# Routed attention and a two-layer network on one Trainium2 core: the up-projection by Strassen's seven products, its left factors streamed from memory

## The chip, the core and the metric

The kernel runs on one NeuronCore of a Trainium2 chip. The core has five engines that run their own instruction streams: TensorE (PE in the profile; its weight loads are listed apart as PEld), VectorE (DVE), ScalarE (ACT), GpSimd (POOL) and SyncE (SP), which here only starts DMA transfers. They meet through semaphores. The metric is the device time of one execution in microseconds. The kernel before took 1125.86 us (median of three runs, 1125.33 to 1126.34).

## What is computed

Inputs are q, k, v of shape (4 batches, 8 heads, 768 rows, 64), 16 centroids for each head, and two weight matrices, w_in (512 x 2048) and w_out (2048 x 512), which arrive as 64-bit floats.

```python
q_assign = argmax(q_n @ c_n.T); k_assign = argmax(k_n @ c_n.T)      # q, k, centroids normalized
scores   = where(q_assign == k_assign, q @ k.T / sqrt(64), -1e9)
attn     = softmax(scores) @ v                                       # per batch and head
x        = attn.transpose(0, 2, 1, 3).reshape(3072, 512)
h        = x @ w_in
g        = h - tanh(h)
out      = g @ w_out                                                 # (3072, 512)
```

## The kernel before, in words

All work is in 32-bit floats. The 3072 tokens are eight **blocks** of 384 (a batch, `b`, and a half of its rows, `half`). Heads go in pairs `p` (4 pairs of 2 heads, one above the other in the 128 partitions). For a block the attention is 12 **steps**: 4 pairs by 3 thirds `s` of the keys; 96 steps in all, in the order of `steps` (line 445). The program is written in its final order by hand: what stands first in the code stands first in each engine's queue.

A step k emits the following (loop from line 524):

- `begin` (line 489): the scores of step k+1, two tiles j0 and j1 (128 keys each, both heads), each followed by an exponential on ACT that overwrites the tile in PSUM (`score`, line 317). The two tiles take both buffers of the pool `ps_s`.
- `value` (line 350): the products of step k's weights with v; in a pair's last third `total` (line 377) multiplies the weights' sum with ones on PE (the tile `den`), which needs the sums that POOL keeps (`sum`, lines 344 and 348).
- items of the **fill**: the network of the block before. `ffn_items` (line 406) gives 16 items `up` (four matmuls over the 512 inputs, 128 x 384 each, then tanh on ACT and `h - tanh` on DVE, line 422) and 12 items `project` (four matmuls of 128 x 512, line 428). The last block's network has no attention beside it and runs alone at the end (lines 568 to 572).
- the list `todo` of the step, cut in equal parts over the slots `between` that each item offers: the two `select` of step k+1 (DVE compares codes and multiplies, line 335; two instructions a tile; the second one also emits POOL's sums), then now and then the transposes of a coming pair (`turn`, line 238, which uses the same two `ps_s` buffers), `divide` (the reciprocal of the sums, line 399), `weights_on`, `route` and `publish` (the arg-max codes).

`weights_on` first turns the 64-bit weights to 32 bits (32 pieces, lines 117 to 125; one piece a step in block 0, three a step in block 1), and then loads each piece again to test its smallest value (line 165). The weights stay in SBUF. Loads of q, k and v go through SP, 8 transfers outstanding at most; the weights' loads go through POOL.

The 16 `up` of a block come in its first six steps (3, 3, 3, 3, 2, 2 to a step), the 12 `project` in the last six, two to a step. Blocks are numbered from 0; in the profile block 2 runs from 265.7 to 391.9 us, and in it the network of block 1.

Of the kernel before, what the change touches and what calls it, by code (L numbers as in the profile page):

```python
# [28 lines left out]
F32 = mybir.dt.float32  # L29
BF16 = mybir.dt.bfloat16  # L30
I32 = mybir.dt.int32
U32 = mybir.dt.uint32
ALU = mybir.AluOpType
# [3 lines left out]
P = 128  # L37
# [14 lines left out]
def kernel(  # L52
# [10 lines left out]
    nc = tc.nc  # L63
# [30 lines left out]
    wholes = const.tile([P, TB], F32, name="wholes")  # L94
    smallest = const.tile([P, len_pieces], F32, name="smallest")
    flag = const.tile([1, 1], I32, name="flag")
    w_in = [const.tile([P, CD, FQ * P], F32, name=f"w_in{i}") for i in range(NQ4)]
    w_out = [const.tile([P, FQ, DM], F32, name=f"w_out{i}") for i in range(NQ4)]

    out_r = out.rearrange("(b p j) m -> b j p m", p=P, j=NCH)  # L100
# [1 line left out]

    w_in_r = moe_w_in.rearrange("(c p) f -> p c f", p=P)
    w_out_r = moe_w_out.rearrange("(c p) m -> p c m", p=P)
    PIECES = [
        (w_in[i][:, c], w_in_r[:, c, i * FQ * P * words : (i + 1) * FQ * P * words])
        for i in range(NQ4) for c in range(CD)
    ] + [(w_out[c // FQ][:, c % FQ], w_out_r[:, c]) for c in range(CF)]

    def assemble(dst, raw, rest):  # L110

# [13 lines left out]
        nc.vector.tensor_tensor(out=bits, in0=bits, in1=rest, op=ALU.add)  # L125

    def fast():
        loads = cx.enter_context(tc.tile_pool(name="loads", bufs=2))
        vp = cx.enter_context(tc.tile_pool(name="vp", bufs=4))
        turnp = cx.enter_context(tc.tile_pool(name="turnp", bufs=4))  # L130
        rtp = cx.enter_context(tc.tile_pool(name="rtp", bufs=1))
        codep = cx.enter_context(tc.tile_pool(name="codep", bufs=6))
        qbp = cx.enter_context(tc.tile_pool(name="qbp", bufs=4))
        ep = cx.enter_context(tc.tile_pool(name="ep", bufs=2))
        sump = cx.enter_context(tc.tile_pool(name="sump", bufs=2))
        xp = cx.enter_context(tc.tile_pool(name="xp", bufs=2))
        rawp = cx.enter_context(tc.tile_pool(name="rawp", bufs=3))
        thp = cx.enter_context(tc.tile_pool(name="thp", bufs=2))
        gp = cx.enter_context(tc.tile_pool(name="gp", bufs=4))
        outp = cx.enter_context(tc.tile_pool(name="outp", bufs=2))  # L140
        ps_s = cx.enter_context(tc.tile_pool(name="ps_s", bufs=2, space=PSUM))
        ps_a = cx.enter_context(tc.tile_pool(name="ps_a", bufs=1, space=PSUM))
        ps_f = cx.enter_context(tc.tile_pool(name="ps_f", bufs=3, space=PSUM))

        raws = {}

        def fetch_weights(n: int):
# [7 lines left out]
        def round_weights(n: int):  # L155
            if words == 1:
                return
            rest = outp.tile([P, FQ * P], U32, name="rest", tag="osb")
            assemble(PIECES[n][0], raws.pop(n), rest)

        def check_weights(n: int):
# [61 lines left out]
        def load(n: int, what=(0, 1)):  # L223
            if n >= len(pairs):
                return
            b, p = pairs[n]
            for i in what:
                if i < 2:
                    t = raw_qk[n, i] = loads.tile([P, NCH, 2, D], F32, name=f"x{i}")
                else:  # L230
                    t = vals[n] = vp.tile([P, 2, NCH, D], F32, name="vals")
                for h in range(2):
                    nc.sync.dma_start(
                        t[:, :, h] if i < 2 else t[:, h],
                        (q, k, v)[i][b, 2 * p + h].rearrange("(p j) d -> p j d", p=P),
                    )
# [166 lines left out]
                nc.gpsimd.tensor_tensor(out=inverses, in0=inverses, in1=dens.pop((n, half)), op=ALU.add)  # L403


        def ffn_items(b: int, half: int):
            gs, acc = [], {}

            def up(f: int, between):
                i, o = f // FQ, f % FQ  # L410
                if o == 0:
                    gs.append(gp.tile([P, FQ, TB], F32, name="g"))
                h = ps_f.tile([P, TB], F32, name="h", tag="f")
                for c in range(CD):
                    nc.tensor.matmul(  # L415
                        h, lhsT=w_in[i][:, c, o * P : (o + 1) * P], rhs=xT[b, half][:, c],
                        start=(c == 0), stop=(c == CD - 1),
                    )
                th = thp.tile([P, TB], F32, name="th")
                nc.scalar.activation(out=th, in_=h, func=ACT.Tanh)  # L420
                between()
                nc.vector.tensor_tensor(out=gs[i][:, o], in0=h, in1=th, op=ALU.subtract)  # L422

            def project(sub: int, i: int, between):
                if i == 0:
                    acc[sub] = ps_f.tile([P, DM], F32, name="o", tag="f")
                for o in range(FQ):
                    nc.tensor.matmul(  # L428
                        acc[sub], lhsT=gs[i][:, o, sub * P : (sub + 1) * P], rhs=w_out[i][:, o],
                        start=(i == 0 and o == 0), stop=(i == NQ4 - 1 and o == FQ - 1),  # L430
                    )
                between()
                if i == NQ4 - 1:
                    osb = outp.tile([P, DM], F32, name="osb")
                    nc.scalar.copy(out=osb, in_=acc.pop(sub))  # L435
                    nc.gpsimd.dma_start(out_r[b, half * HCH + sub], osb)  # L436

            return [lambda between, f=f: up(f, between) for f in range(CF)] + [
                lambda between, s=s, i=i: project(s, i, between)
                for s in range(HCH) for i in range(NQ4)  # L440
            ]

# [6 lines left out]

        def before(n: int):  # L450

            yield lambda: (turn(n, 0, nc.scalar), turn(n, 1, nc.scalar), load(n + 2))
            yield lambda: similar(n)
            yield lambda: route(n)
            yield lambda: publish(n)
# [17 lines left out]
        def fetch():  # L473
            nonlocal fetched
            if fetched < (1 if words == 1 else 2) * len(PIECES):
                fetch_weights(fetched % len(PIECES))
                fetched += 1

        def weights_on():

            nonlocal done
            if done < len(PIECES):
                round_weights(done)
            elif done < 2 * len(PIECES) and words == 2:
                check_weights(done - len(PIECES))
            done += 1
            fetch()

        def begin(step):
            n, half, s = step  # L490
            for i in range(2):
                score(n, half, 2 * s + i)

        centroid_load()
        load(0)
        for i in range(3):
            fetch()
        constants()
        load(1)
        load(0, (2,))  # L500
        for n in range(1, HP):
            load(n, (2,))
        turn(0, 0, nc.scalar)
        turn(0, 1, nc.vector)
        centroid_norms()
        similar(0)
        turn(1, 0, nc.scalar)
        load(2)
        route(0)
        publish(0)  # L510
        spread(0, 0)
# [3 lines left out]
        for i in range(2):  # L515
            select(*steps[0][:2], i)
        turn(1, 1, nc.scalar)
        load(3)
        similar(1)
        route(1)  # L520
        publish(1)

        late = []
        for at, (n, half, s) in enumerate(steps):
            b, p = pairs[n]
            following = steps[at + 1] if at + 1 < len(steps) else None
            after = steps[at + 2] if at + 2 < len(steps) else None
            block = 2 * b + half
            if p == 0 and s == 0:
                fill = ffn_items((block - 1) // 2, (block - 1) % 2) if block else []  # L530
            left = HP * NS - (p * NS + s)
            now = [fill.pop(0) for _ in range(-(-len(fill) // left))]
            stages = dict(ready.get(at, []))
            if 1 in stages:
                stages[1]()
            if after and after[2] == 0:
                spread(*after[:2])
            if following:
                begin(following)
            value(n, half, s)  # L540
            if s == NS - 1:
                total(n, half)
                late += [lambda n=n, half=half, i=i: divide(n, half, i) for i in range(HCH)]
                if half == 1:
                    load(n + HP, (2,))

            todo = []
            if following:
                todo += [lambda i=i: select(*following[:2], 2 * following[2] + i) for i in range(2)]
            if 0 in stages:  # L550
                todo.append(stages[0])
            todo += late
            late = []
            todo += [weights_on] * (3 if block == 1 and done < len(PIECES) else 1)
            todo += [stages[i] for i in (2, 3) if i in stages]
            slots = max(len(now), 1)
            for i in range(slots):
                mine = todo[i * len(todo) // slots : (i + 1) * len(todo) // slots]

                def between(mine=mine):  # L560
                    for it in mine:
                        it()

                if i < len(now):
                    now[i](between)
                else:
                    between()
        fill = ffn_items(B - 1, 1)
        for it in late:
            it()  # L570
        for it in fill:
            it(lambda: None)


        for t, bound in ((inverses, MOST_INVERSE), (wholes, SUM_MOST)):
# [16 lines left out]
    def general():  # L592
# [3 lines left out]
        identb = gs.tile([P, P], BF16, name="identb")  # L596
        nc.vector.tensor_copy(out=identb, in_=ident)

        for dst, src in PIECES if words == 2 else ():
            raw = gs.tile([P, 2 * FQ * P], U32, name="graw")  # L600
            nc.sync.dma_start(raw, src)
            rest = gs.tile([P, FQ * P], U32, name="grest")
# [165 lines left out]
```

## Time and profile before

| | |
|---|---|
| median of three runs | 1125.86 us |
| the profiled execution, its own time | 1126.44 us |
| its span (first to last instruction) | 1124.5 us |
| PE busy | 1063.1 us, 95% |
| DVE, ACT, POOL busy | 509.9, 304.7, 377.9 us |
| matmuls of `up` (line 415) | 344.0 us |
| matmuls of `project` (line 428) | 341.0 us |
| DMA, mean | 59 GB/s |

How to read it: the page cuts the span into 40 slices and gives each engine's busy share of a slice in tenths. A float matmul goes through PE in two passes and is listed as two instructions, each with a weight load of its own. `x24` after an operation is a count of such instructions that were merged in one row. In a row of the timeline the first number is the start, the second the length in us; in square brackets stands the engine's idle time ahead of it and what ended it. The view by windows gives busy us and instruction counts of each engine in a stretch, then the clock that PE was granted (1.00 is full), and the share of the DMA engines.

### The profile page before, as it was taken

The numbers are of one execution on the slowest core, as the hardware profiler recorded it, in microseconds if no ns is written. First come the engines' busy times: TensorE is split into PE (matmuls) and PEld (weight loads), VectorE is DVE, ScalarE is ACT, GpSimd is POOL, SyncE is SP. The second block draws the span as 40 slices with busy tenths as digits, with TensorE's granted clock in tenths as the row PEclk, the third lists the DMA queues.
The fourth block names the chain that finished last, engine by engine and source line by source line (L and its number), as shares of the span: only waits on it lengthen the run. The fifth ranks groups of instructions, "written<-read, shape, count | busy, mean of one in ns | idle before, by whom it ended". The sixth has DMA issues, their size and how long they took to land.

```text
span 1124.5 us, 10709 instructions
## 1 busy us (share of the span) xinstructions
PE 1063.1 (95%) x3922; PEld 500.6 (45%) x3922; DVE 509.9 (45%) x893; ACT 304.7 (27%) x491; POOL 377.9 (34%) x298
## 2 busy tenths in 40 slices
PE   3776998999999999999999999999999999999996
PEld 2332444444544455444554445444554445444542
DVE  3578899534553344444543234443343334432210
ACT  2333334322322223222332223313332122211100
POOL 1012344443353433434234333343334433442000
PEclk9988999999999999999999999999999999999999
DMA  7442256433222123331100002110000000000000
GB/s 197 122 115 77 78 158 183 139 98 92 79 64 66 63 64 88 91 104 62 36 29 10 10 9 50 38 43 30 12 28 10 24 10 1 1 10 19 1 9 22
DMA packets 71115, 65.86 MB, mean 59 GB/s; under 512 B 53136, under 2 KB 61328, under 8 KB 71056
## 3 DMA queue, kind: packets, MB, share of 16 engines
q0 software_dynamic: 11136, 39.85, 11.1%
q1 hardware_dynamic: 59776, 25.22, 9.1%
q8 instruction: 33, 0.54, 0.2%
q14 instruction: 26, 0.21, 0.1%
q10 hardware_dynamic: 144, 0.03, 0.0%
HBM read 58.75 MB, written 6.34 MB: 58 GB/s over the span
## 4 chain that ended last, share of the span: by engine, by line
PE 78%; issue 9%; DVE 9%; DMA 1%; ACT 1%; POOL 1%; SPq 0%; POOLq 0%; DVEq 0%; ACTq 0%
PE o L428 26%; PE h L415 23%; PE sc L321 12%; PE av L357 11%; PE sim L261 2%; DVE e L335 2%; PE den L385 1%; DVE w_out L122 1%; PE pt L243 1%; DVE den L399 1%; ACT t L249 1%; PE den L366 1%; DMA x<-in_k_dram 1%; DVE w_out L125 1%; DVE w_out L118 1%
## 5 line engine op out<-in xcount | busy, mean ns | idle before, releaser
L415 PE MATMUL h<-xT,w_in 128*128 128x384 f32 x1024 | 344.0, 492 | 5.8 <-DVE top L282 4.0
L428 PE MATMUL o<-w_out,g 128*128 128x512 f32 x768 | 341.0, 598 | 0.0
L335 DVE SCALAR_TENSOR_TENSOR e<-row,code,sc 128x384 f32<-128x384 bf16 x384 | 211.7, 607 | 254.4 <-ACT sc L326 195.7
L348 POOL TENSOR_TENSOR sum<-sum,e 128x768 f32<-128x768 f32 x112 | 202.5, 1808 | 260.1 <-DVE e L335 257.4
L415 PEld LDWEIGHTS h<-xT,w_in 128*128 128x128 f32 x1024 | 191.6, 191 | 157.1 <-issue 19.2
L428 PEld LDWEIGHTS o<-w_out,g 128*128 128x128 f32 x768 | 142.4, 190 | 188.5 <-issue 183.4
L326 ACT ACTIVATE sc<-sc 128x768 f32<-128x768 f32 x192 | 144.4, 793 | 208.4 <-PE sc L321 194.2
L321 PE MATMUL sc<-t,t 64*128 64x384 f32 x768 | 155.8, 524 | 5.8 <-DVE e L335 5.5
L422 DVE TENSOR_TENSOR g<-h,th 128x384 f32<-128x384 f32 x128 | 71.0, 554 | 184.3 <-ACT th L420 184.0
L357 PE MATMUL av<-e,vals 128*64 128x384 f32 x768 | 148.5, 508 | 0.0
L420 ACT ACTIVATE th<-h 128x384 f32<-128x384 f32 x128 | 62.7, 490 | 300.6 <-PE h L415 298.5
L321 PEld LDWEIGHTS sc<-t,t 64*128 64x128 f32 x768 | 68.1, 191 | 83.8 <-issue 56.6
L399 DVE RECIPROCAL den<-den 128x128 f32<-128x128 f32 x96 | 84.0, 919 | 35.6 <-POOL wholes L393 35.6
L357 PEld LDWEIGHTS av<-e,vals 128*64 128x64 f32 x768 | 47.4, 138 | 89.9 <-issue 87.2
L393 POOL TENSOR_TENSOR wholes<-wholes,den 128x384 f32<-128x384 f32 x32 | 31.8, 993 | 139.3 <-ACT den L392 139.3
L436 POOL DMA_DIRECT2D out_dram<-osb x24 | 13.3, 553 | 156.5 <-ACT osb L435 156.5
L403 POOL TENSOR_TENSOR inverses<-inverses,den 128x384 f32<-128x384 f32 x32 | 43.7, 1364 | 63.4 <-DVE den L399 63.4
L435 ACT COPY osb<-o 128x512 f32<-128x512 f32 x24 | 14.1, 588 | 168.6 <-PE o L428 168.6
L344 POOL TENSOR_TENSOR sum<-e 128x768 f32<-128x768 f32 x28 | 50.4, 1802 | 5.1 <-DVE e L335 5.1
L153 POOL DMA_DIRECT2D raw<-in_moe_w_in_dram x32 | 18.3, 571 | 88.7 <-DVE w_in L122 60.1
L249 ACT COPY t<-pt 128x768 f32<-128x768 f32 x31 | 23.5, 801 | 69.9 <-PE pt L243 69.9
L243 PE MATMUL pt<-ident,x 128*128 128x128 f32 x192 | 27.0, 293 | 15.4 <-DMA x<-in_q_dram 9.6
(67 smaller groups left out, 372.2 us busy)
## 6 DMA issues: line engine op xcount, KB each, us to landing
raw<-in_moe_w_in_dram POOLq DMA_DIRECT2D x32, 512.0 KB, 4.3
raw<-in_moe_w_out_dram POOLq DMA_DIRECT2D x32, 512.0 KB, 4.0
x<-in_q_dram SPq DMA_DIRECT2D x32, 192.0 KB
x<-in_k_dram SPq DMA_DIRECT2D x32, 192.0 KB
vals<-in_v_dram SPq DMA_DIRECT2D x32, 192.0 KB
row<-q_codes SPq DMA_DIRECT2D x32, 192.0 KB
out_dram<-osb POOLq DMA_DIRECT2D x24, 256.0 KB, 2.3
q_codes<-qc SPq DMA_DIRECT2D x16, 3.0 KB
```

The costliest lines, as they stand in the source:

```text
L321: nc.tensor.matmul(sc[:, h, 0:TB], lhsT=turned[n, 1][r].rearrange("p a n -> p (a n)")[:, j * P : (j + 1) * P], rhs=turned[n, 0][r, half], ...
L326: nc.scalar.activation(out=sc[:, :, 0:TB], in_=sc[:, :, 0:TB], func=ACT.Exp, scale=SCALE)
L335: nc.vector.scalar_tensor_tensor(out=e[:, h], in0=rows[n, half][:, h], scalar=codes[n][:, 1, j // HCH, h, j % HCH : j % HCH + 1], in1=sc[: ...
L344: nc.gpsimd.tensor_tensor(out=s, in0=pair[:, 0], in1=pair[:, 1], op=ALU.add)
L348: nc.gpsimd.tensor_tensor(out=s, in0=s, in1=pair[:, i], op=ALU.add)
L357: nc.tensor.matmul(avs[n, half][h * D : h * D + D], lhsT=vals[n][:, h, j], rhs=e[:, i, h], start=(j == 0), stop=(j == NCH - 1),)
L399: nc.vector.reciprocal(out=t[:, c], in_=t[:, c])
L403: nc.gpsimd.tensor_tensor(out=inverses, in0=inverses, in1=dens.pop((n, half)), op=ALU.add)
L415: nc.tensor.matmul(h, lhsT=w_in[i][:, c, o * P : (o + 1) * P], rhs=xT[b, half][:, c], start=(c == 0), stop=(c == CD - 1),)
L420: nc.scalar.activation(out=th, in_=h, func=ACT.Tanh)
L422: nc.vector.tensor_tensor(out=gs[i][:, o], in0=h, in1=th, op=ALU.subtract)
L428: nc.tensor.matmul(acc[sub], lhsT=gs[i][:, o, sub * P : (sub + 1) * P], rhs=w_out[i][:, o], start=(i == 0 and o == 0), stop=(i == NQ4 - 1 ...
```

## The change

For the blocks 1 to 7 the up-projection is done on quarters. Two outputs f and f+8 of 128 features each and the two halves of the block's 384 tokens (192 each) make a 2 x 2 product, and the 512 inputs are halved. Seven products of (128 outputs) x (256 inputs) x (192 tokens) replace eight. The seven left factors (four of them sums of quarters of w_in) are made once, in block 1 after the weights are done, by DVE; they are written to DRAM and read back by SP, one tile `stream` of 7 KB a partition for each pair of outputs, three pairs ahead. Four differences of the quarters of x are made by DVE at each block's end. So an item `up_pair` holds 14 matmuls of 128 x 192 in place of 8 of 128 x 384; the products are put together by one copy on ACT and four additions on DVE, with tanh on ACT and the subtraction now on POOL. Block 0's network still uses `up`, with one buffer for tanh's result where there were two.

The fill is dealt out by estimated cost (2.6 for `up`, 4.6 for `up_pair`, 3.4 for `project`) in place of item counts. An `up_pair` offers two slots to `todo`, one ahead of its last two products' addition and one at its end. Buffers are rearranged: q and k of batch 0 sit in the buffers of g and are all loaded at the start; later ones have one buffer in place of two and are loaded one pair ahead; `row` has three buffers in place of four. At the start the identity is made ahead of the first weight loads on POOL. The second reading of the weights starts at block 2 (before: in block 1).

```diff
+        def keep_factor(q: int, which: int, t):
+            for c in range(CH):
+                nc.sync.dma_start(
+                    factors[q * FQ : (q + 1) * FQ, :, which, c].rearrange("i p f -> p i f"),
+                    t[:, c].rearrange("p (i f) -> p i f", f=P),
+                )
+        def factor_items(q: int):
...
+            return [
+                lambda: (make(S1, a21, a22, ALU.add), keep_factor(q, A11, a11)),
+                lambda: (make(S3, a11, a21, ALU.subtract), keep_factor(q, A12, a12)),
+                lambda: (make(S2, S1, a11, ALU.subtract), keep_factor(q, S1, made[S1])),
+                lambda: (keep_factor(q, S3, made[S3]), make(S4, a12, S2, ALU.subtract)),
+                lambda: (keep_factor(q, S2, made[S2]), keep_factor(q, A22, a22)),
+                lambda: keep_factor(q, S4, made[S4]),
+            ]
+        def fetch_factors(k: int):
+            if k < (2 * B - 1) * HF:
+                t = streams[k] = wp.tile([P, 7, CH, P], F32, name="stream", tag="w")
+                nc.sync.dma_start(t, factors[k % HF])
+        def differences(b: int, half: int):
...
+            for i, (u, w) in enumerate(((b12, b11), (b22, d[:, 0]), (b22, b12), (b21, d[:, 1]))):
+                nc.vector.tensor_tensor(out=d[:, i], in0=u, in1=w, op=ALU.subtract)
...
+            def up_pair(i: int, between):
...
+                m = mixp.tile([P, 8, N], F32, name="mix", tag="mix")
+                ps = ps_f.tile([P, N], F32, name="p1", tag="f")
+                product(ps, A11, x[:, 0:CH, 0:N])
+                nc.scalar.copy(out=m[:, 7], in_=ps)
+                ps = ps_f.tile([P, 2, N], F32, name="p26", tag="f")
+                product(ps[:, 0], A12, x[:, CH:CD, 0:N])
+                product(ps[:, 1], S2, d[:, 1])
+                nc.vector.tensor_tensor(
+                    out=m[:, 0:7:6], in0=ps, in1=m[:, 7:8].to_broadcast([P, 2, N]), op=ALU.add
+                )
+                ps = ps_f.tile([P, 2, N], F32, name="p75", tag="f")
+                product(ps[:, 0], S3, d[:, 2])
+                product(ps[:, 1], S1, d[:, 0])
+                nc.vector.tensor_tensor(out=m[:, 5], in0=ps[:, 0], in1=m[:, 6], op=ALU.add)
+                nc.vector.tensor_tensor(
+                    out=m[:, 3:5], in0=ps[:, 1:2].to_broadcast([P, 2, N]), in1=m[:, 5:7], op=ALU.add
+                )
+                between()
+                ps = ps_f.tile([P, 2, N], F32, name="p34", tag="f")
+                product(ps[:, 0], S4, x[:, CH:CD, N:TB])
+                product(ps[:, 1], A22, d[:, 3])
+                nc.vector.tensor_tensor(out=m[:, 1:3], in0=ps, in1=m[:, 4:6], op=ALU.add)
+                nc.scalar.activation(out=m[:, 4:8], in_=m[:, 0:4], func=ACT.Tanh)
+                g = gs[i] = gp.tile([P, 2, TB], F32, name="g")
+                nc.gpsimd.tensor_tensor(
+                    out=g.rearrange("p a n -> p (a n)"),
+                    in0=m[:, 0:4].rearrange("p a n -> p (a n)"),
+                    in1=m[:, 4:8].rearrange("p a n -> p (a n)"), op=ALU.subtract,
+                )
+                fetch_factors((block - 1) * HF + i + 3)
+                between()
...
+            if block == 0:
+                ups = [(2.6, 1, lambda between, f=f: up(f, between)) for f in sequence]
+            else:
+                ups = [(4.6, 2, lambda between, i=i: up_pair(i, between)) for i in range(HF)]
...
-        centroid_load()
         load(0)
+        centroid_load()
+        constants()
         for i in range(3):
             fetch()
-        constants()
         load(1)
         load(0, (2,))
-        for n in range(1, HP):
-            load(n, (2,))
+        load(1, (2,))
+        for n in range(2, HP):
+            load(n, (0, 1, 2))
...
-            left = HP * NS - (p * NS + s)
-            now = [fill.pop(0) for _ in range(-(-len(fill) // left))]
+                whole, spent = sum(it[0] for it in fill), 0.0
+            now = []
+            part = (p * NS + s + 1) / (HP * NS)
+            while fill and (spent + fill[0][0] / 2 <= whole * part or part == 1):
+                now.append(fill.pop(0))
+                spent += now[-1][0]
...
-            todo += [weights_on] * (3 if block == 1 and done < len(PIECES) else 1)
+            if block == 1 and done >= len(PIECES):
+                if not makers and at < HP * NS * 2 - 1:
+                    makers = factor_items(0) + factor_items(1)
+                    makers += [lambda i=i: fetch_factors(i) for i in range(3)]
...
+            else:
+                todo += [weights_on] * (3 if block == 1 else 1)
             todo += [stages[i] for i in (2, 3) if i in stages]
-            slots = max(len(now), 1)
+            slots = max(sum(it[1] for it in now), 1)
```

Here CH, N and HF are 2 chunks of inputs, 192 tokens and 8 pairs of outputs; `d` holds the four differences.

## The prediction

> **What bounds the kernel now.** I read the page's busy line and slices first, then the view by windows, then the timeline of single steps.
>
> ```profile
> PE 1063.1 (95%) x3922; PEld 500.6 (45%) x3922; DVE 509.9 (45%) x893; ACT 304.7 (27%) x491; POOL 377.9 (34%) x298
> ...
> PE   3776998999999999999999999999999999999996
> ```
>
> PE is at nine tenths from slice 7 on. By windows (the stretch and its length; busy PE, PEld, DVE, ACT, POOL; PE's clock), the first half of block 1 and then block 4:
>
> ```profile
> 124.60:197.40 72.80, 66.73 (x258) 33.74 (x256) 67.67 (x104) 29.28 (x51) 36.22 (x33) 0.98 0.47 140
> ...
> 525.00:651.20 126.20, 125.97 (x459) 58.98 (x458) 51.39 (x88) 33.43 (x54) 47.08 (x31) 1.00 0.08 21
> ```
>
> DVE holds the first (93% busy); PE alone holds the second, idle 0.23 us of 126.2. So after 265 us each PE microsecond saved counts, and each wait of PE too. The timeline of step 28 shows how waits are covered today:
>
> ```profile
> 313.37 1.56 PE L321 MATMUL sc<-t,t 64*128 64x384 f32 x8
> ...
> 314.33 1.50 ACT L326 ACTIVATE sc<-sc 128x768 f32<-128x768 f32 x2 [0.37 <-PE sc L321]
> ...
> 315.23 1.14 DVE L335 SCALAR_TENSOR_TENSOR e<-row,code,sc 128x384 f32<-128x384 bf16 x2 [0.67 <-ACT sc L326]
> ...
> 316.30 5.43 PE L415 MATMUL h<-xT,w_in 128*128 128x384 f32 x16
> 316.53 1.80 POOL L348 TENSOR_TENSOR sum<-sum,e 128x768 f32<-128x768 f32 x1 [3.09 <-DVE e L335]
> 319.19 0.49 ACT L420 ACTIVATE th<-h 128x384 f32<-128x384 f32 x1 [3.35 <-PE h L415]
> ```
>
> Scores and values take 2.93 us (313.37 to 316.30), then come two `up`. The select of tile j0 runs at 315.23, beside `value`: nothing of the network stands ahead of it on DVE. Both score buffers are free long before PE returns for the next scores.
>
> **PE's saving.** A pass of 384 columns takes 0.322 us (the last block's 128 passes in 41.3 us), one of 512 takes 0.429 (16 to 6.86), so 0.835 ns a column; the line through both gives 0.162 for 192 columns. An `up_pair` is 28 passes, 4.54 us, against 16 passes, 5.16: 0.62 saved, times 56, **-34.7 us**. The cover needed is that the weight load fits in the pass:
>
> ```profile
> 50.93 1.29 PEld L243 LDWEIGHTS pt<-ident,x 128*128 128x128 f32 x12 [0.60 <-issue]
> 50.93 1.53 PE L243 MATMUL pt<-ident,x 128*128 128x128 f32 x12
> ```
>
> Here 128-column loads start 0.11 us apart, though each lasts about 0.15. A load for a float matmul lasts 0.19 (page, line 415). Ends: 0.162 if loads overlap as here, 0.190 if they don't (a pair 5.3). I take 0.162.
>
> **The wait that is added.** In the changed program's order of DVE, an `up_pair` is: first add (p26), second and third (p75), then slot 1 of `todo`, then the fourth add (p34), then slot 2. So the selects of the next step now queue behind three adds that wait for PE's p75. The third add has no wait for PE of its own, so the second's must cover both p75 products. Queued behind the selects are PE's next scores, which need the two `ps_s` buffers.
>
> Let T be the end of p75. PE runs p34 until T+1.30. DVE starts at T+0.20 (PE to ACT: 316.30+0.11+2.58 to 319.19). Second add 0.37 (estimate, 192 elements, from 0.56 us at 384 and 0.68 at 512), third 0.56, select j0 1.13 to T+2.26, select j1 to T+3.39. PE resumes with scores j0 at T+2.32 (waits 1.02) and, 0.65 later, waits 0.48 for j1: **1.5 us**. If `todo` has only three entries, halving it puts select j1 behind the fourth add: T+4.01, **2.1 us**.
>
> This bites in steps with a single `up_pair`. Dealing 77.6 units over 12 steps (6.47 each) gives 1, 2, 1, 2, 1 pairs, then a pair with a project, then projects alone. In a step of two pairs the first takes the selects early; with three entries select j1 still stands behind the second pair's p75, 0.4. Steps 0 to 4 of the six blocks 2 to 7:
> - step 0: 2.1 in odd blocks. In 2, 4, 6 `turn` comes after the pair: its transposes wait 1.0 and 0.4 for the two buffers, its ACT copies queue behind the pair's tanh, the `sim` matmuls wait 1.7 for them; 3.1, of which before already shows 0.2: 2.9.
> - step 1: 0.4 in odd blocks.
> - step 2: 1.5 (divides make `todo` long).
> - step 3: 0.4, except in 3 and 5, whose `todo` has four entries.
> - step 4: 2.1; in 3 and 5, where `route` lengthens `todo` and fills 0.4, 1.1.
>
> **A second wait, on POOL.** `den` (PE, steps 2 and 5) needs POOL's sums. POOL now subtracts tanh (768 elements, 1.81 by the row of line 348), and in step 4 of blocks 2, 4, 6, 7 that stands ahead of both sums: from the step's start, select j0 ends 8.55, fourth add 9.14, tanh 10.03, subtraction 11.9, sums 15.5. PE, already late, comes to `den` at 12.3: 3.25. Elsewhere 0.6 or less: in step 1 of even blocks the subtraction is ahead too, but a second pair hides most; in step 4 of 3 and 5 the sums are ahead.
>
> Sums: even blocks 2.9+0.6+1.5+0.4+2.1+3.25 = 10.75 each; 3 and 5: 2.1+0.4+1.5+1.1+0.55 = 5.65; block 7: 2.1+0.4+1.5+0.4+2.1+3.25 = 9.75. Total **+53.3 us**, over 18 single steps. If the second add starts at p75's first product, 0.36 goes from each single step: -6.5.
>
> **The clock.** The four waits of 3.25 us have a neighbour in block 0, on the timeline:
>
> ```profile
> 114.10 1.98 PE L321 MATMUL sc<-t,t 64*128 64x384 f32 x8 [3.20 <-DVE e L335]
> ```
>
> and, by windows, PE's clock (0.50, third from the end) just behind it:
>
> ```profile
> 115.90:119.30 3.40, 3.40 (x14) 1.27 (x14) 3.26 (x7) 1.36 (x2) 0.53 (x1) 0.50 0.41 126
> ```
>
> After 3.20 us idle PE is granted half clock for 3.4 us, which costs 1.7. Four times: **+6.8**; ends 0, and 12 if the three `turn` steps do it too.
>
> [...]
>
> **The rest.**
> - DVE: 2.05 us of adds a pair for 1.11 of subtractions, and four differences (2.2) a block. Before the next pair needs them there are two projects and the scores (10 us) against 4.3 to the divides' end and 5.6 more: nothing. DVE stays near 55%, POOL near 43%. PE's gaps hide no more.
> - Streams: 917 KB, fetched three pairs (over 13 us) ahead; 512 KB land in 4.3 us, so some 7.5. Cover: those pairs. A `row` transfer behind one on SP has a step to land. 0, at worst 5 a block, 30.
> - Block 1: DVE-bound as before; the single tanh buffer makes ACT wait for DVE's subtraction, which adds some gaps; the eight factors (1.2 us each, from the same line) and their 28 stores on SP run beside projects, with the weight checks moved out. +1.5 (-2 to 6; the stretch's non-DVE time is 5.1).
> - Start: POOL makes the identity (0.6 us) before its weight transfers, so q's first transfer runs alone longer; the last q and k no longer share with the first `row`. DVE waits 1.49 for that row. -1 (-2.5 to 1, for the added early loads).
> - End: pairs without attention. Each add, tanh and subtraction has 4.5 us; nothing waits.
>
> Sum: -34.7 + 53.3 + 6.8 + 0.5 = **+25.9 us**. The profiled execution took 1126.44 (span 1124.5 and 1.94 around it), 0.58 above the median: 1152.3 on its own time, **1152** against the median 1125.86.
>
> **Rivals.**
> - *Only the selects' wait, and shorter* (faster). The second add starts at p75's first product, and POOL's sums come in time. Without the `den` waits (15.9) and the clock (6.8), with 6.5 less: 1152-29 = 1123; with half the select waits still hidden, 1108. Place: DVE between p75 and the next scores. It decides where all waits together fall below 34 us, 1.9 for each single-pair step. For it: POOL's and DVE's rates leave them half idle on average. Against: the order, in which both stand behind the pair. If PE waits nowhere, 1091.
> - *The weight load becomes the bound* (slower): 28 times 0.190 is 5.3, so +9 for -34.7: some 1190. Against: the transposes above.
> - *Streams or `row` late*: up to +30 more, 1180. For: `row` comes behind 917 KB. Against: three pairs of lead.
> - *No seven products where said*: block 0 keeps `up`, but 56 pairs stand in the built order, 14 matmuls each; ruled out.
>
> **How the numbers follow.** What this kernel's measurement tells from no change is about 0.2%, 2.25 us. Forecast, 1130 to 1172: 65%. First rival: 24%, spread 1091 to 1130, of which 19 faster (under 1123.6), 4 the same, 1 slower. Weight load 5%, streams 6%, both slower. Faster 0.19, same 0.04, slower 0.77. The unknown ends give 1152 less 6.5 (second add), 6.8 (clock) and 5 (block 1, start), so 1134, and 1152 plus 5.2 (clock) and 6.5 (block 1, start), so 1164, or 1172 with a quarter of the streams' 30. Downward the range goes on to 1115, which takes in the upper half of the first rival and leaves out some 10%; above 1172 lie some 8%.
>
> **What would show it.** `up_pair`'s passes 0.162 apart in the last block (36.3 us for eight pairs). In blocks 2 to 7, PE idle ahead of the scores, released by DVE's select, 1.5 to 2 us in steps 0, 2 and 4; ahead of `den`, released by POOL's sum, 3 us four times; half clock after these. With the clock, blocks 2, 4 and 6 about 7.5 us longer than before, 7 about 6.5, 3 and 5 about 0.7; the end 5 shorter. I'd be wrong if single-pair steps show PE without idle time, or passes at 0.19.

## The result, and the profile after

The changed kernel took 1143.59 us (median of four executions, 1139.63 to 1147.1), the kernel before 1126.09 beside it. The ratio is 1.0156, 95% interval 1.0119 to 1.0193: slower by 17.5 us. The profiled execution is the fastest of the four, 1139.63, with a span of 1137.9 against 1124.5: **+13.4**. The working below is against this one.

The page of the changed kernel, its busy line and its slices of PE and of PE's clock:

```profile
PE 1041.1 (91%) x4594; PEld 586.1 (52%) x4594; DVE 603.4 (53%) x1041; ACT 308.4 (27%) x491; POOL 479.3 (42%) x354
...
PE   3776988999989999999989999999989999899996
...
PEclk8788999999999999999999999999998999999998
```

PE is busy 22 us less than before (1063.1), and yet the span is longer. In the slices after the tenth, where before showed 9 alone, there are now single 8s: PE waits, four times in the same manner. PE's waits by cause (us in total, times, the longest):

```profile
PE sc L328 <- DVE e L342: 21.4, 26, 4.2
...
PE den L392 <- POOL sum L355: 13.5, 7, 3.1
...
PE sim L268 <- ACT t L256: 5.3, 10, 1.2
...
PE pt L250 <- DVE e L342: 2.9, 6, 0.8
```

Before, the first of these was 5.5 us, all of it ahead of block 2, and the second was not there. After the change, 6.3 of the 21.4 lie ahead of block 2, the longest wait among them. What the first two rows have behind that are the selects and the sums that the prediction queued behind the pair; the last two rows are mostly the steps with `turn`. The timeline of the same stretch as before (step 28 of block 2 into step 29):

```profile
320.25 0.81 PE L492 MATMUL p<-xT,stream 128*128 128x192 f32 x4
...
320.45 0.36 DVE L511 TENSOR_TENSOR mix<-p,mix 128x192 f32<-128x192 f32 x1 [0.67 <-PE p L492]
...
320.84 0.56 DVE L512 TENSOR_TENSOR mix<-p,mix 128x384 f32<-128x384 f32 x1
...
321.32 1.13 DVE L342 SCALAR_TENSOR_TENSOR e<-row,code,sc 128x384 f32<-128x384 bf16 x2
...
322.50 0.92 PE L328 MATMUL sc<-t,t 64*128 64x384 f32 x4 [0.79 <-DVE e L342]
322.83 1.13 DVE L342 SCALAR_TENSOR_TENSOR e<-row,code,sc 128x384 f32<-128x384 bf16 x2
...
323.94 1.80 POOL L522 TENSOR_TENSOR g<-mix 128x768 f32<-128x768 f32 x1 [5.14 <-ACT mix L520]
...
324.02 0.92 PE L328 MATMUL sc<-t,t 64*128 64x384 f32 x4 [0.60 <-DVE e L342]
...
325.71 3.67 POOL L355 TENSOR_TENSOR sum<-sum,e 128x768 f32<-128x768 f32 x2
...
329.44 0.87 PE L392 MATMUL den<-sum,ones 128*64 128x384 f32 x4 [3.06 <-POOL sum L355]
```

Read it from the second add (L511): it waits for PE's p75, the third add follows, and only then the selects (L342), for which PE's scores wait twice. POOL subtracts (323.94), then sums until 329.38; `den` is released by that, 3.06 us late.

The weight loads were no bound. The first pairs of the last block, on the timeline:

```profile
1051.10 1.98 PEld L492 LDWEIGHTS p<-diff,stream 128*128 128x128 f32 x12
1051.26 2.11 PE L492 MATMUL p<-diff,stream 128*128 128x192 f32 x12
```

Twelve loads start within 1.98 us less the last one's 0.19, so 0.163 apart, which is the 192-column pass of the forecast.

By stretches, each from the first scores of the step that opens it:

| stretch | before | after | change |
|---|---|---|---|
| start to block 2 | 265.7 | 266.05 | +0.3 |
| blocks 2, 3, 4, 5 | 126.13, 133.17, 126.13, 133.17 | 130.20, 132.10, 130.18, 132.11 | +4.1, -1.1, +4.1, -1.1 |
| block 6 | 126.13 | 133.17 | +7.0 |
| block 7 up to its last two steps | 101.97 | 107.11 | +5.1 |
| the rest: two steps and the last network | 112.03 | 106.96 | -5.1 |

The forecast had some 7.5 for blocks 2, 4 and 6, 0.7 for 3 and 5, 6.5 for 7, and -5 for the end.

Blocks 2, 4 and 6 have the same instructions, but block 6 takes 3 us more. The windows of the step after the `den` wait, in block 4 and in block 6 (window and length; busy PE, PEld, DVE, ACT, POOL; PE's clock; DMA share):

```profile
584.80:600.70 15.90, 12.24 (x58) 7.26 (x58) 7.19 (x14) 4.47 (x7) 8.31 (x6) 1.00 0.50 166
847.10:866.00 18.90, 15.24 (x58) 9.68 (x58) 6.61 (x13) 4.47 (x7) 7.83 (x5) 0.82 0.32 109
853.40:860.20 6.80, 6.20 (x19) 5.02 (x20) 0.41 (x1) 0.81 (x2) 1.53 (x2) 0.50 0.00 0
```

The same 58 matmuls; the difference of 3.0 us is half clock, granted for 6.8 us in block 6 (third line) and not at all in block 4, after a wait of 3.06 us in both.

### The profile page after: what moved, and what is told of

Same layout as the page of the kernel before. It is cut to its first block, busy times and chain, and to the rows that moved or that the text cites. A ratio compares the mean times of both kernels' runs of the same rounds, so it can differ in the third digit from the quotient of the medians.

```text
span 1137.9 us, 12514 instructions
## 1 busy us (share of the span) xinstructions
PE 1041.1 (91%) x4594; PEld 586.1 (52%) x4594; DVE 603.4 (53%) x1041; ACT 308.4 (27%) x491; POOL 479.3 (42%) x354
## 3 DMA queue, kind: packets, MB, share of 16 engines
q0 software_dynamic: 11136, 39.85, 10.6%
## 5 line engine op out<-in xcount | busy, mean ns | idle before, releaser
L342 DVE SCALAR_TENSOR_TENSOR e<-row,code,sc 128x384 f32<-128x384 bf16 x384 | 211.2, 607 | 168.5 <-ACT sc L333 112.0
L328 PE MATMUL sc<-t,t 64*128 64x384 f32 x768 | 162.1, 532 | 22.8 <-DVE e L342 21.4
L492 PE MATMUL p<-diff,stream 128*128 128x192 f32 x896 | 164.9, 327 | 0.0
L522 POOL TENSOR_TENSOR g<-mix 128x768 f32<-128x768 f32 x56 | 102.3, 1827 | 127.0 <-ACT mix L520 126.9
L492 PEld LDWEIGHTS p<-diff,stream 128*128 128x128 f32 x896 | 149.8, 191 | 0.0
L492 PE MATMUL p<-xT,stream 128*128 128x192 f32 x672 | 133.5, 336 | 0.0
L492 PEld LDWEIGHTS p<-xT,stream 128*128 128x128 f32 x672 | 112.3, 193 | 23.2 <-issue 16.0
L505 DVE TENSOR_TENSOR mix<-p,mix 128x384 f32<-128x384 f32 x56 | 31.2, 557 | 166.8 <-PE p L492 101.4
L520 ACT ACTIVATE mix<-mix 128x768 f32<-128x768 f32 x56 | 47.2, 843 | 260.7 <-DVE mix L519 260.7
L543 POOL DMA_DIRECT2D out_dram<-osb x24 | 13.4, 557 | 110.1 <-ACT osb L542 107.8
```

Source lines behind the costliest of these rows:

```text
L328: nc.tensor.matmul(sc[:, h, 0:TB], lhsT=turned[n, 1][r].rearrange("p a n -> p (a n)")[:, j * P : (j + 1) * P], rhs=turned[n, 0][r, half], ...
L342: nc.vector.scalar_tensor_tensor(out=e[:, h], in0=rows[n, half][:, h], scalar=codes[n][:, 1, j // HCH, h, j % HCH : j % HCH + 1], in1=sc[: ...
L492: nc.tensor.matmul(out, lhsT=w[:, which, c], rhs=right[:, c], start=(c == 0), stop=(c == CH - 1),)
L520: nc.scalar.activation(out=m[:, 4:8], in_=m[:, 0:4], func=ACT.Tanh)
L522: nc.gpsimd.tensor_tensor(out=g.rearrange("p a n -> p (a n)"), in0=m[:, 0:4].rearrange("p a n -> p (a n)"), in1=m[:, 4:8].rearrange("p a n ...
```

## Experiments

**Theory W**: PE's saving is there, and it is outweighed by what PE waits for: selects behind the pair's adds on DVE, and sums behind the subtraction on POOL, each with its own place in the code. **Rival G**: the added work on DVE, POOL and the queues costs what it costs wherever it stands. The runs move instructions, and leave the work as it is, except where it is said.

### sums_first: the second slot ahead of POOL's subtraction

```diff
                 nc.scalar.activation(out=m[:, 4:8], in_=m[:, 0:4], func=ACT.Tanh)
+                between()
                 g = gs[i] = gp.tile([P, 2, TB], F32, name="g")
...
-                between()
```

> Only the second slot of an up_pair is moved: ahead of POOL's subtraction (it stood behind it), so POOL's sums go before the subtraction. Theory W (the lost time is PE's waits for what stands behind the pair on DVE and POOL): the four waits of 3.06 us ahead of den and the two of 0.43 go (-13), and with them the half clock behind them (-4.6 in the profile); the waits for the selects stay (about 29 us). Time 1126, 1121 to 1132. Rival G (the added adds, subtractions and transfers cost time wherever they stand): 1140 to 1147.

Measured: 1122.49 us (before 1124.92), ratio 0.9978 (0.9969 to 0.9988). The same step on its timeline:

```profile
323.90 3.71 POOL L355 TENSOR_TENSOR sum<-sum,e 128x768 f32<-128x768 f32 x2 [3.71 <-DVE e L342]
...
327.67 0.87 PE L392 MATMUL den<-sum,ones 128*64 128x384 f32 x4
...
328.15 1.82 POOL L523 TENSOR_TENSOR g<-mix 128x768 f32<-128x768 f32 x1
```

The sums stand first, `den` doesn't wait, and behind it there is no half clock in any block. One line moved on POOL is worth 21 us of medians, and 16 between the profiled executions: the four large `den` waits and their half clock. The two of 0.43 in blocks 3 and 5, which W also let go, are still there (0.45 and 0.44). PE still waits 21.6 us for DVE's selects, as before this edit.

### select_early: the first slot behind p1

```diff
                 nc.scalar.copy(out=m[:, 7], in_=ps)
+                between()
...
-                between()
                 ps = ps_f.tile([P, 2, N], F32, name="p34", tag="f")
```

> Only the first slot of an up_pair is moved: right behind the copy of p1, ahead of the three adds, so select j0 (and j1 where todo has four entries) no longer queues behind p75. Theory W: waits for score buffers fall from about 29 us to some 10 (select j1 still stands behind the fourth add where todo has three entries); the four waits ahead of den stay at about 3 us, some with half clock behind. Time 1122, 1116 to 1130. Rival G: 1140 to 1147.

Measured: 1122.13 us, ratio 0.9967 (0.9955 to 0.998). Its timeline:

```profile
319.48 0.92 PE L328 MATMUL sc<-t,t 64*128 64x384 f32 x4
...
321.25 0.92 PE L328 MATMUL sc<-t,t 64*128 64x384 f32 x4 [0.85 <-DVE e L342]
...
326.68 1.41 PE L392 MATMUL den<-sum,ones 128*64 128x384 f32 x4 [3.08 <-POOL sum L355]
328.01 2.67 PE L492 MATMUL p<-xT,stream 128*128 128x192 f32 x8
```

The first scores wait no more, the second ones once, 0.85, where select j1 is in the slot behind the pair. The `den` wait is untouched, and the passes behind it run at half clock (2.67 us for eight, against 1.57). So the two waits are separate, and the two edits are worth about the same, 21 us of medians each.

### slots_early: both

```diff
                 nc.scalar.copy(out=m[:, 7], in_=ps)
+                between()
...
                 fetch_factors((block - 1) * HF + i + 3)
-                between()
```

> Both slots are moved: the first behind the copy of p1, the second to where the first was (behind the third add, ahead of p34). Selects and sums are then ahead of the fourth add, tanh and the subtraction. Theory W: nearly all of the 47 us of waits go, 2 to 5 us are left: time 1100, 1096 to 1106, faster than the kernel before. Rival G: 1140 to 1147.

The first slot stands behind p1, the second behind the third add. Measured: 1093.10 us (1092.54 to 1093.98), ratio 0.972 (0.9704 to 0.9737). PE's waits from block 2 on come to 3.5 us, of the 2 to 5 expected. In direction this is W; the time is 3 us below its range. The 1100 is the median less 47 us of waits plus what is left: it has no term for the half clock that goes with the waits (4.6 us in the profile), nor for the five steps with `turn`, which are some 1.0 us shorter each (see below). G, at 1140 to 1147, is out: in blocks 2 to 7 the same work costs next to nothing where PE doesn't stand behind it.

### two_pairs: slots as in the changed kernel, the pairs dealt two to a step

```diff
+            kk = p * NS + s
+            count = (2 if kk < 4 else 1 + kk % 2) if block > 1 else None
-            while fill and (spent + fill[0][0] / 2 <= whole * part or part == 1):
+            while fill and (
+                len(now) < count if count else spent + fill[0][0] / 2 <= whole * part or part == 1
+            ):
```

In blocks 2 to 7 the steps 0 to 3 take two pairs each, the others one or two projects.

> The slots stay as in the changed kernel; only the dealing differs in blocks 2 to 7: two up_pairs in each of steps 0 to 3, then 1, 2, 1, 2 ... projects. No step has a single pair, so half of todo goes behind the first pair and PE has the second pair to run meanwhile. Theory W: left are 0.4 us at the end of steps with three entries, 5 to 10 us in all, no wait over 1.5 us and no half clock: time 1104, 1099 to 1111. Rival G: 1140 to 1147, as no instruction is added or taken away.

Measured: 1090.05 us (1089.81 to 1090.76), ratio 0.9693 (0.9677 to 0.9709), the best with th2 below. Its busy line, and a stretch of its timeline:

```profile
PE 1028.0 (94%) x4594; PEld 584.0 (54%) x4594; DVE 593.7 (55%) x1041; ACT 307.4 (28%) x491; POOL 479.2 (44%) x354
```

```profile
321.19 2.19 DVE L342 SCALAR_TENSOR_TENSOR e<-row,code,sc 128x384 f32<-128x384 bf16 x4 [1.08 <-ACT sc L333]
321.39 3.70 PE L534 MATMUL o<-w_out,g 128*128 128x512 f32 x8
...
325.02 1.56 PE L328 MATMUL sc<-t,t 64*128 64x384 f32 x8
...
327.86 0.81 PE L392 MATMUL den<-sum,ones 128*64 128x384 f32 x4
```

POOL's busy time is that of the changed kernel (479.3 there), DVE's within 10 us of it (603.4); step 28 holds two projects, the selects run beside them, and neither the scores nor `den` wait. PE's gaps from block 2 on add up to 0.9 us. I had expected 1104, and 1099 at the least, with 0.4 left in each step of two pairs. There 0.2 is left, too little to be shown in brackets (the first scores and the first values of the next step start 1.71 apart in place of 1.49), 2.5 us in all. What the expectation lacks besides is the same as in slots_early. A block takes 120.65 or 127.73 us: -5.5 against before, of which eight pairs make 4.9 and the step with `turn` 1.0, less 0.4 of small waits.

### double_subtract: POOL's subtraction done twice

```diff
+                for _ in range(2):
                     nc.gpsimd.tensor_tensor(
```

The second one writes the same result again; only POOL's time grows, by 1.8 us a pair.

> The changed kernel with POOL's subtraction of each up_pair done twice (the same values written again), everything else as in the changed kernel. Theory W: the wait ahead of den in step 4 to 5 of blocks 2, 4, 6 and 7 grows from 3.06 to 4.9 us (+7.3 in all), a new one of up to 1.3 us comes in step 1 to 2 of the even blocks, and each gap over 3.4 us brings half clock (in the changed kernel's profile two of four gaps of 3.06 did): 1152 to 1160. If POOL's subtraction is not what den waits for: within 3 us of the changed kernel.

Measured: 1165.88 us, ratio 1.0355 (1.0338 to 1.0373), 22 us over the changed kernel's median, some 6 more than the most that W gave. Its timeline in the same step:

```profile
328.06 3.70 POOL L523 TENSOR_TENSOR g<-mix 128x768 f32<-128x768 f32 x2 [1.50 <-ACT mix L520]
...
331.72 3.68 POOL L355 TENSOR_TENSOR sum<-sum,e 128x768 f32<-128x768 f32 x2
...
335.45 1.55 PE L392 MATMUL den<-sum,ones 128*64 128x384 f32 x4 [4.96 <-POOL sum L355]
```

The large wait grew from 3.06 to 4.96, by one subtraction, as W has it. What W missed: the `den` of step 2 now waits as well, 2.03 us in even blocks (1.3 expected) and 1.34 in the blocks 3, 5 and 7 (none expected), and eight periods of half clock follow, two of them behind gaps of 2.03 us alone. Each of the four gaps of 4.96 us had half clock behind it, as did each gap over 3.4 us from 60 us on in before (5.20, 5.25 and 3.98 us) and in the changed kernel's first profile (5.20, 5.25, 4.17 and 3.99).

### both: two pairs to a step and early slots

Its edit is that of two_pairs with that of slots_early.

> two_pairs and slots_early together. Theory W: two_pairs has 0.9 us of PE gaps over 0.15 us left after block 2's start, so there is nothing more to take: 1090, 1088 to 1092. If the slots' place also cost time in another way than by these waits: 1085 or less.

Measured: 1103.93 us (1100.39 to 1105.58), ratio 0.9816 (0.98 to 0.9831): a miss, worse than either edit alone. Its timeline in step 2 of block 2:

```profile
303.80 1.75 DVE L406 RECIPROCAL den<-den 128x128 f32<-128x128 f32 x2
...
305.34 0.27 PE L303 MATMUL pq<-ident,code 128*12 128x128 f32 x1
305.58 1.53 DVE L409 TENSOR_TENSOR xT<-xT,den 128x384 f32<-128x384 f32 x1
...
307.04 0.54 DVE L506 TENSOR_TENSOR mix<-p,mix 128x384 f32<-128x384 f32 x1
...
307.64 0.92 PE L492 MATMUL p<-xT,stream 128*128 128x192 f32 x4 [2.02 <-DVE mix L506]
```

The slot behind p1 holds `divide` here: two reciprocals and a product of 1.53 us stand ahead of the pair's first add (L506), and `publish`'s tile `pq` has taken a buffer of `ps_f`, so p34 waits for the add to empty p26: 2.02 us. An early slot brings the selects forward, and everything else of `todo` too; the wait has moved from the scores to the pair itself. This is in three blocks, 6.1 us; the even blocks are 2.3 longer than in two_pairs (block 6 by 3.9, with one period at half clock), 3 and 5 by 0.7 and 0.4. With block 7's 0.2 that is 9.9 of the 10.6 us between the ends of the two profiled executions; the others of this kernel took up to 5 us more, and have no trace.

### th2: two buffers for tanh's result in block 0's network

```diff
+                ths = diffp.tile([P, 2, TB], F32, name="th", tag="diff")
-                th = diffp.tile([P, TB], F32, name="th", tag="diff")
+                th = ths[:, f % 2]
```

On top of two_pairs.

> two_pairs with tanh's result of block 0's network double-buffered again (two halves of the one tile). Block 1 took 144.1 us in two_pairs and 143.0 in the changed kernel, against 141.1 before. If the single tanh buffer is the cause, block 1 falls to about 141.5 and the time to 1087.5; if the factors (eight DVE additions, 28 stores) are, it stays at 143 to 144 and the time at 1090.

Measured: 1089.83 us (1089.3 to 1092.57), ratio 0.9694 (0.9681 to 0.9708), not to be told from two_pairs. Block 1 went from 144.09 to 142.88 in the profiles (before the change 141.13), so the single buffer is at most 1.2 of the 3.0 us there. Since the changed kernel's block 1 varied by 0.9 among the executions below, even that isn't settled.

### again_1 to again_4: the changed kernel, four more executions

Why half clock after two of four equal waits? In every trace of this case the stretches at half clock start whole multiples of 3.413 us apart (in double_subtract 297.5, 335.0, 570.5, 608.1, 877.7 and 1007.5: 11, 80, 91, 170 and 208 periods after the first, the last one 710.0 us after it). **Theory M**: the clock is granted by such periods. **Rival R**: the length of the gap decides.

> The changed kernel itself, once more. Theory M (the clock is granted by periods of 3.413 us that run on through the whole execution, on their own phase: a period in which PE is busy about 1.4 us or less is followed by one at half clock, one with 1.82 or more never is): the four waits ahead of den are 3.06 us again, but how many of them are followed by half clock depends on where they fall in the periods, so that the number changes from execution to execution, all half-clock stretches start a whole number of 3.413 us apart, and the span is 1133.3 us plus 1.6 to 3.1 us for each of the stretches behind a wait: 1133 to 1146. Rival R (the gap's length alone decides): every execution has its half clock behind the same waits, those of blocks 6 and 7, and the span is 1137 to 1139.

For the second (the third and fourth have the same words):

> As for again_1: by theory M another number of half-clock stretches, each start on the grid of 3.413 us within its execution, the span 1133.3 us plus 1.6 to 3.1 for each stretch behind a wait; by R the same two stretches and 1137 to 1139.

Measured, each from its own profile; PE's waits are the same in all (21.4 to 21.5 for the selects, 13.5 to 13.6 for the sums):

| execution | time | periods at half clock behind the `den` wait of block 2, 4, 6, 7 | length of blocks 2, 4, 6 |
|---|---|---|---|
| the first profile | 1139.63 | 0, 0, 2, 1 | 130.20, 130.18, 133.17 |
| again_2 | 1139.78 | 0, 0, 2, 1 | 130.21, 130.23, 133.15 |
| again_4 | 1142.00 | 1, 0, 2, 1 | 131.81, 130.18, 133.20 |
| again_3 | 1142.80 | 1, 0, 2, 1 | 131.76, 130.19, 133.18 |
| again_1 | 1146.53 | 2, 1, 2, 1 | 133.13, 131.85, 133.06 |

A block's length goes by its number of periods alone: none 130.2, one 131.8, two 133.1. So one costs 1.6 us and two 2.9. The spans are 1138.0 to 1144.8 us: R's 1137 to 1139 holds for again_2 only, M's 1133 to 1146 for all four. The spread of the changed kernel is this and what lies ahead of block 2, where again_1 takes 2.5 us more than the first profile, again_3 1.6 and again_4 0.7. What decides is seen in windows laid on the periods. The first profile, block 4 and then block 6:

```profile
587.18:590.59 3.41, 1.47 (x10) 0.44 (x8) 0.00 (x0) 1.27 (x2) 3.33 (x3) 1.00 0.45 168
590.59:594.01 3.42, 2.30 (x13) 1.70 (x14) 0.00 (x0) 0.81 (x2) 2.39 (x3) 1.00 0.33 71
850.01:853.42 3.41, 0.93 (x6) 0.14 (x2) 0.00 (x0) 0.81 (x2) 3.33 (x3) 0.99 0.32 118
853.42:856.83 3.41, 2.83 (x8) 1.65 (x9) 0.00 (x0) 0.49 (x1) 1.20 (x2) 0.50 0.00 0
856.83:860.25 3.42, 3.42 (x12) 3.42 (x12) 0.46 (x1) 0.32 (x1) 0.32 (x1) 0.51 0.00 0
```

And again_1, block 4:

```profile
594.10:597.51 3.41, 0.34 (x2) 0.20 (x4) 0.00 (x0) 0.48 (x1) 3.33 (x3) 0.98 0.07 22
597.51:600.92 3.41, 3.41 (x12) 2.47 (x9) 0.00 (x0) 0.81 (x2) 1.11 (x2) 0.51 0.57 154
```

A wait of 3.06 us that a boundary cuts in two leaves PE 1.47 us of work in the first period and 2.30 in the second: full clock goes on. The same wait within one period leaves 0.93 or 0.34, and the next period is at half clock.

## Why the forecast came out as it did

Direction and mechanism were right, the size was 8 us too large: +25.9 forecast, +17.5 by the medians, +13.4 in the profiled execution.

- **PE's saving**: forecast -34.7. The passes are 0.163 apart, and the last network's eight pairs take 36.4 us (36.3 by the forecast) where they took 41.3, 4.9 saved (5.0 by the forecast). Right, and none of it was lost to weight loads. That two_pairs comes out 34.9 below before agrees with the forecast in part by chance: its profile is 36.4 shorter, some 34.0 by passes and 5.0 by `turn`, less 2.5 of small waits and 0.3 ahead of block 2.
- **The two waits**: both are where they were put, with the releasers named. The step that failed in size is the price of a single wait. The sum lays DVE's rows end to end from T, the end of p75's passes, and has PE back at T+1.30. In the rows above T is 320.25: the scores start at T+2.25 where the forecast had 2.32, their second half at T+3.77 where it had 4.01, since each of DVE's instructions starts some 0.08 before the row ahead of it ends. And PE isn't back at T+1.30: a step of two projects lasts 10.00 in before, from scores to scores, its rows of scores and values take 2.93 and its 16 passes 6.86, so that 0.2 is left over in any case, about half of it ahead of the scores; in steps of the changed kernel without this wait the scores start at T+1.39.
- **Each price**, by the starts on PE, with the forecast in brackets: a select 0.86 (1.02, and about as much again for the second), so two selects 1.7 (2.1), in step 4 of blocks 3 and 5 0.9 (1.1); step 2 1.2 to 1.3 (1.5); a step of two pairs 0.2 (0.4); `turn`'s step 2.4 (2.9); the large `den` wait 3.3 by the starts, 3.06 in its row (3.25).
- **What the sum overlooked**: `turn` costs 3.08 us of a step in before (13.95 for 10.87 in step 0 of block 2), and 2.09 where products of a pair stand between its transposes and `sim`: the eight `sim` matmuls then take 0.78 us up to the next scores, where they take 1.47 right behind ACT's copies. In the changed kernel this is so in step 3 of blocks 3 and 5 and gives back 2.0 in all. Waits less this gain: even blocks 8.9 (10.75), 3 and 5 3.8 (5.65), 7 8.4 (9.75); in all **42.6 for 53.3**.
- **The clock**: forecast 6.8, four times 1.7. A stretch costs 1.6 for a period and 2.9 for two; the profiled execution has three periods, 4.6 us, the others three to six, 4.6 to 9.1. The price was right; that every such gap is followed by one was not: it depends on where the gap falls. The range of 0 to 12 held it; no profile of the changed kernel came below 4.6.
- **Start and block 1**: forecast +0.5, measured +0.3 (block 1 +1.85, the start and block 0 -1.5). What of block 1's part is due to the factors and what to the single buffer stays open.
- **Streams and `row`**: nothing; a stream lands in 5.2 us (7.5 estimated), and no PE wait after block 2 is for a transfer.

Sum for the profiled execution: -34.0 (29.1 in the loop and 4.9 behind it) + 42.6 + 4.6 + 0.3 = +13.5, measured +13.4. The waits were taken as what a step's length leaves above its passes, so that this sum closes nearly of itself; the independent support is in the runs that take each wait away.

The rival "only the selects' wait" didn't happen, but sums_first makes one of its two conditions true, POOL's sums in time: 1122.5, where the rival had 1123 to 1108. The other, a second add that starts at p75's first product, did not come true in any run (L511 waits for PE 0.67 us in the rows above). The rival with the weight load adds up to 1196 by its own terms, not 1190; its passes at 0.19 were not seen.

## What to carry to other kernels

When work is moved onto engines that are half idle, go through what stands behind it in each engine's order, for the one engine that is full: here 35 us of fewer matmuls turned into a loss of 17, and became a gain of 35 when the pairs were dealt two to a step, so that the same instructions had other PE work beside them. A slot that moves one urgent instruction forward moves all others in it; look at the longest of them before moving it. And where a few gaps like the ones here remain, expect a spread of times, not one time: with the same waits, up to 3.06 us ahead of `den`, the changed kernel's profiled spans were 1137.9 to 1144.8 us.

## What the runs showed of the hardware

- Half clock was granted in periods of 3.413 us that kept their grid through an execution: in the changed kernel's first profile it starts at 112.69, 187.78, 853.38 and 983.09, which is 22, 217 and 255 periods after the first. Lay the periods on the starts of half clock: in blocks 2 to 7 of all traces, each of the 24 at full clock in which PE was busy 1.39 us or less was followed by a period at half clock, and none with 1.44 or more was. In blocks 0 and 1 the line is less sharp: in again_3 a period of 1.58 us was followed by full clock (from 184.17) and one of 1.69 by half (from 112.49), so that busy time alone doesn't settle it there. A period at half clock that was busy 3.32 us or more was followed by full clock in blocks 2 to 7, one with 2.99 or less by another at half.
- So a gap of 2.03 us can cost 1.7 us of clock (double_subtract: busy 1.38 and 1.39 in the period; step 2 takes 13.1 us in blocks 2 and 4, 11.4 in block 6), and one of 3.06 us may cost none. The length of a gap alone doesn't settle it.
- Around the network's passes PE takes some 0.2 us that no row shows as a wait (10.00 us for a step, 6.86 of passes and 2.93 of rows). About half lies ahead of the scores: in before, the 24 passes of a step with three `up` last 7.94 us up to the scores, and 7.84 up to `turn`'s transposes.
- `turn`'s eight `sim` matmuls take 0.78 us, from the first to the scores behind them, where both of ACT's copies are done before PE comes to them (two_pairs, step 0 of block 2), and 1.47 where PE waits for the copies (before, the same step).
